# A planned kernel: keeping VectorE and GpSimd apart on their shared port, in the plan and by semaphores

## The chip, the cores and the metric

The kernel runs on one core of one Trainium2 chip. The metric is the device time of one execution in microseconds (us). The profile's span, from first to last instruction, is about 2 us shorter than that time. In the first call, whose chip the record does not name, the runs of one kernel lie within 0.5%. The experiments ran on two chips, called the second and the third below, which were noisier, so small differences are given with 95% intervals. A run more than 1.5% above the fastest of its kernel is called slow.

## The reference, cut to what matters

An attention with a decaying state makes `y`; reshaped to 3072 rows of 384, it is the input of a feed-forward block.

```python
for t in range(S):                                   # B=4, H=8, S=768, D=48
    cur = einsum('bhd,bhe->bhde', u[None] * kt, vt)
    y[:, :, t] = einsum('bhd,bhde->bhe', rt, state + cur)
    state = w[None, :, :, None] * state + einsum('bhd,bhe->bhde', kt, vt)
x = y.transpose(0, 2, 1, 3).reshape(B * S, H * D)    # 3072 x 384
h = x @ w_in                                         # 384 x 2048
r = maximum(h, 0.0); g = r * r
out = g @ w_out                                      # 2048 x 384
```

## The kernel before

The kernel cuts attention into 24 units of 128 steps (6 stretches of the sequence, 4 batches). Per unit, five elementwise products of 128x384 (`kw`, `rw`, `rk`, `rku`, `dv`, and a smaller `smo`) may run on VectorE or on GpSimd. Two units feed one of 12 feed-forward pairs: eight groups of six matmuls for the first product ("first products"), a relu, a square, and then groups of four matmuls of the second ("second products").

The order of instructions on every engine is not written by hand. A planner, which is Python that runs when the kernel is built, gives each operation a start, an engine and a place in that engine's queue, from assumed durations. The chip keeps the order of each queue, but not the planned times: an instruction starts as soon as it is first in its queue and its operands are there.

The port rule of the planner before, the fitted priorities and one product:

```python
s = max(t, free[e])
if e == "V" and o.port and lastP is not None and lastP[1] > s:
    s = lastP[1]
elif e == "P" and lastV is not None and lastV[2] and lastV[1] > s >= lastV[0]:
    s = lastV[1]
late = s + o.swift * cost + (away if i else 0.0)
...
if o.dma is not None:
    ...
    if e == "P":
        lastP = (s, s + 0.3, False)
...
ORDER = {"kvm": 1.49, "m1": -2.25, "m2": 0.04, ...}      # added to every operation's key
EARLY = {"dv": -1.05, "relu": 13.78, "trk": -22.02, ...} # added in the first units alone
AWAY, SWIFT, SWIFT_UNITS = 0.05, 1.0, 10
...
q["rku"] = op(f"rku{n}", both(0.96, 0.48), K + 2, [q["rk"], o_ub], ..., port=True)   # GpSimd 0.96, VectorE 0.48
...
for o in placed:
    ...
    o.emit(o.by)
```

`port=True` marks products with both inputs in SBUF, the memory that the engines share. When VectorE has such a product while GpSimd has one too, one of them takes longer (1.35 instead of 0.55 us in the trace below); that is called a collision, an overlap or a port conflict here. The rule looks at the last operation of the other engine only: once VectorE has been given another operation, an earlier port product is forgotten.

Of the kernel before, what the change touches and what calls it, by code (L numbers as in the profile page):

```python
# [11 lines left out]
ALU = mybir.AluOpType  # L12
# [3 lines left out]
class Op:  # L16


    def __init__(self, name, eng, key, deps, takes, emit, lat, port, dma):
        self.name, self.eng, self.key, self.deps, self.takes = name, eng, key, deps, takes  # L20
        self.emit, self.lat, self.port, self.dma = emit, lat, port, dma
        self.start = self.end = self.by = self.ins = None
        self.gap, self.swift = 0.0, 0.0


class Buf:
# [8 lines left out]
        return max(u.end for u in self.users) + 0.1  # L35


def schedule(ops, depth, limits, free, away, stalls, warm_until=0.0):
    rings = {r: [] for r in depth}
    banks = [None] * 8  # L40
    free = dict(free)
# [6 lines left out]
            succ.setdefault(d, []).append(o)  # L48
    ready = [o for o in ops if need[o] == 0]
    placed = []  # L50
    lastP = lastV = None
    base, queue = {}, []

    def ring_time(o):
# [49 lines left out]
    while ready:  # L104
        best = None
        for o in ready:
            t = base.get(o)
            if t is None:
                t = 0.0
                for d, lat in o.deps:  # L110
                    t = max(t, d.end + (d.lat if lat is None else lat))
                base[o] = t
            if best is not None and t > best[0][0]:
                continue
            r = ring_time(o)
            if r is None:
                continue
            t = max(t, r)
            if best is not None and t > best[0][0]:
                continue  # L120
            chosen = ()
            if any(bf.ring in limits for bf in o.takes):
                got = pick_banks(o, t)
                if got is None:
                    continue
                t, chosen = got
            pick = None
            for i, (e, cost) in enumerate(o.eng.items()):
                s = max(t, free[e])
                if e == "V" and o.port and lastP is not None and lastP[1] > s:  # L130
                    s = lastP[1]
                elif e == "P" and lastV is not None and lastV[2] and lastV[1] > s >= lastV[0]:
                    s = lastV[1]
                late = s + o.swift * cost + (away if i else 0.0)
                if pick is None or late < pick[0]:
                    pick = (late, s, e)
            rank = (pick[1], o.key)
            if best is None or rank < best[0]:
                best = (rank, o, pick[2], chosen)
        if best is None:  # L140
            raise RuntimeError("stuck: " + ", ".join(o.name for o in ready[:20]))
        (s, _), o, e, chosen = best
        cost = o.eng[e]
        o.start, o.by = s, e
        o.gap = s - free[e]
        if o.dma is not None:
            pre, xf, post = o.dma
            x0 = max(s + pre, free["D"])
            x1 = x0 + xf + sum(d for at, d in stalls if x0 <= at < x0 + xf)
            free["D"], o.end = x1, x1 + post  # L150
            free[e] = s + cost
            if e == "S":
                queue.append(x1)
                if len(queue) > 2:
                    free[e] = max(free[e], queue[-3])
            if e == "P":
                lastP = (s, s + 0.3, False)
        else:
            o.end = s + cost
            free[e] = o.end  # L160
            if e == "P":
                lastP = (s, o.end, o.port)
            elif e == "V":
                lastV = (s, o.end, o.port)
        for bf in o.takes:
            if bf.ring not in limits:
                bf.slot = len(rings[bf.ring]) % depth[bf.ring]
                rings[bf.ring].append(bf)
        for bf, i in chosen:
            bf.slot = i  # L170
            banks[i] = bf
        ready.remove(o)
        placed.append(o)
        for n in succ.get(o, ()):
            need[n] -= 1
            if need[n] == 0:
                ready.append(n)
# [6 lines left out]
def kernel(  # L184
# [30 lines left out]
    WARM0 = 5  # L215
    NT = 10
    NDVE = 24
    ORDER = {"kvm": 1.49, "m1": -2.25, "m2": 0.04, "mask": -2.59, "relu": -0.41, "sbo": 5.28, "sma": 3.15, "smo": -0.97, "sq": 1.01, "vb": 4.47, "ym": -0.91, "yt": -4.84}
    EARLY = {"dv": -1.05, "kw": 0.33, "m1": 1.78, "m2": 1.76, "osb": 5.37, "relu": 13.78, "rkT": -3.42, "rku": 0.23, "sma": -6.8, "trk": -22.02, "trr": 5.21, "vb": -6.7, "ym": -10.21, "yt": 2.72}
    AWAY, SWIFT, SWIFT_UNITS = 0.05, 1.0, 10  # L220
    PIECES = (0, 1, 2, 4, 6, 8)
    AHEAD = 4
    BEFORE, BEHIND = 4, 1
# [130 lines left out]

    o_wb = op("wb", {"W": 0.0}, -60, [], lambda e: None, lat=0.75)
    o_row = op("row", {"W": 0.0}, -59, [], lambda e: None, lat=0.0)
    o_ubp = op("ubp", {"T": 1.3}, -58, [o_row], spread_u, takes=[ub_p], lat=0.25)
    o_wcol = op("wcol", {"T": 1.4}, -57, [o_ubp], column_w, takes=[wc_p], lat=0.25)
    o_ln = op("lnw", {"A": 0.5}, -56, [o_wb], lambda e: nc.scalar.activation(lnw, wb, AF.Ln))
    o_wk = op("wk", {"A": 0.5}, -55, [o_ln],  # L360
              lambda e: nc.scalar.activation(wk.rearrange("p h d -> p (h d)"), lnw, AF.Exp, scale=ek))
# [28 lines left out]
    def load(n, nm, gate=None):  # L390
        q = units[n]
        src = {"kt": k, "rt": r, "vt": v}[nm]
        c, b = q["c"], q["b"]

        def f(e):
            q[nm].ins = nc.sync.dma_start(
                out=q["T"](nm), in_=src[b, :, c * C : (c + 1) * C, :].rearrange("h t d -> t h d"))
            if gate is not None:
                tc.add_manual_dep(q[nm].ins.ins, gate.ins.ins.name, LANDED)

        deps = [(gate, 0.05)] if gate is not None else []
        if loads:
            deps.append((loads[-1], -40.0))
        q[nm] = op(f"{nm}{n}", {"S": 0.55}, PACE * (n - AHEAD), deps, f, takes=[q["_" + nm]], lat=0.05, dma=(0.65, 0.95, 1.8))
        loads.append(q[nm])

    o_win, o_wout = [None] * NH, [None] * NH
# [1 line left out]
    def weights(i, which, gate):  # L409
        lo, hi = PIECES[i], PIECES[i + 1]  # L410
        sl = slice(lo * 256, hi * 256) if which == "in" else slice(lo * 2, hi * 2)

        def f(e):
            if which == "in":
                o.ins = nc.gpsimd.dma_start(out=w_in_sb[:, :, sl], in_=w_in_v[:, :, sl])
            else:
                o.ins = nc.gpsimd.dma_start(out=w_out_sb[:, sl, :], in_=w_out_v[:, sl, :])
            if gate is not None:
                tc.add_manual_dep(o.ins.ins, gate.ins.ins.name, LANDED)

        o = op(f"w_{which}{i}", {"P": 0.77}, -5 + 0.1 * i, [(gate, 0.05)] if gate is not None else [(w_ops[-1], -40.0)], f, lat=0.05,
               dma=(1.45, (1.0 if which == "in" else 1.12) * (hi - lo), 1.4))
        for j in range(lo, hi):
            (o_win if which == "in" else o_wout)[j] = o
        return o
# [152 lines left out]
    for j in range(NU // L):  # L578
# [5 lines left out]
        for i, q in enumerate(us):  # L584
            if q["n"] >= NT:
                o_xt.append(op(
                    f"xt{q['n']}", {"S": 1.2}, PACE * q["n"] + 4.4, [q["yb"]],
                    lambda e, XT=XT, i=i, q=q: nc.sync.dma_start_transpose(out=XT()[:, :, i, :], in_=q["T"]("yb")),
                    takes=[xt] if i == 0 else [], uses=[q["_yb"]] + ([xt] if i else []), lat=0.05, dma=(0.9, 0.6, 1.1)))
                continue  # L590
            o_xt.append(op(f"xt{q['n']}", {"A": 0.37, "V": 0.28}, PACE * q["n"] + 4.5, [q["yt"]],
                           copy(lambda XT=XT, i=i: XT()[:, :, i, :], q["ytp"]),
# [6 lines left out]
        for f in range(NH):  # L599
# [22 lines left out]
            def square(e, f=f, gr=gr, G=G):  # L622
                src = make["gr"][gr.slot]
                dst = G()[:, 2 * f : 2 * f + 2].rearrange("p z b t -> p (z b t)")
                if e == "A":
                    nc.scalar.activation(dst, src, AF.Square)  # L626
                else:
                    NOW[e].tensor_tensor(dst, src, src, ALU.mult)  # L628

            o_r = op(f"relu.{j}.{f}", {"V": 0.6, "A": 0.5}, key - 1, [o_m], relu, uses=[gr, h])  # L630
            o_s = op(f"sq.{j}.{f}", {"A": 0.55, "P": 1.02}, key - 1, [o_r], square, uses=[gr, g], port=True)
# [20 lines left out]
    for o in ops:  # L652
        if o.key < PACE * SWIFT_UNITS:
            o.swift = SWIFT

    for o in ops:
        kind, _, num = o.name.partition(".")
        if not num:
            kind, num = o.name.rstrip("0123456789"), o.name[len(o.name.rstrip("0123456789")):]
        elif kind.rstrip("0123456789") == "mask":  # L660
            kind, num = "mask", kind[4:]
        ffn = kind in ("m1", "m2", "relu", "sq")
        first = int((num.partition(".")[0]) or 0) < (3 if ffn else 6)
        o.key += ORDER.get(kind, 0.0) + (EARLY.get(kind, 0.0) if first else 0.0)

    placed = schedule(
        ops, depth, limits,
        free={"T": 4.0, "V": 4.2, "A": 4.4, "P": 2.3, "D": 2.7, "S": 1.2, "W": 3.2},
        stalls=[(18.3 + 12.4 * i, 1.0) for i in range(16)],
        away=AWAY, warm_until=WARM_UNTIL)  # L670
    for o in placed:
        if o.by == "T" and o.gap > 0 and o.start < WARM_UNTIL:
            warm(int(o.gap * WARM_FILL / 0.2133))
        o.emit(o.by)


# [28 lines left out]
```

## Time and profile before

| | before |
|---|---|
| time | 182.15 us median of 3 runs (182.13 to 182.28) |
| span of the profiled run | 181.0 us (its time was 183.06 us) |
| TensorE, VectorE, GpSimd busy | 93%, 78%, 61% |
| first first-product, first second-product | 22.1 us, 38.8 us |
| port products on VectorE | 28, of which 17 pairs overlap a GpSimd product |

The head of the profile page of the kernel before: busy us of each engine, then busy tenths in 40 slices of 4.5 us, and the granted TensorE clock in tenths.

```profile
span 181.0 us, 4349 instructions
...
PE 168.6 (93%) x1646; PEld 122.0 (67%) x1646; DVE 141.6 (78%) x257; ACT 111.4 (62%) x221; POOL 110.6 (61%) x131
...
PE   6995698999999989999999898999999999999992
...
PEclk9999879999999999999999999999999999999999
```

After about 40 us TensorE is practically always busy. The idle time is in the ramp, slices 4 and 5 (about 14 to 23 us), where the granted clock falls a little later. The Trainium skill, "TensorE: Matmul & The Clock Gate", section "What's actually happening", says that a hardware activity monitor sets the clock by how busy TensorE has been. This trace agrees: the stretches view gives a granted clock of 0.66 for 20 to 25 us, at the end of the idle slices and just after, and 1.00 for the next 5 us.

The timeline of VectorE (DVE) and GpSimd (POOL) in the ramp of the kernel before: start us, duration us, engine, line, operation, result and inputs.

```profile
11.71 0.69 DVE L332 TENSOR_TENSOR krp<-rt,wr 128x384 bf16<-128x384 f32 x1
12.32 1.35 DVE L332 TENSOR_TENSOR rku<-rk,ub 128x384 f32<-128x384 f32 x1
...
17.70 0.97 DVE L332 TENSOR_TENSOR krp<-rt,wr 128x384 bf16<-128x384 f32 x1
...
19.83 1.06 DVE L332 TENSOR_TENSOR rku<-rk,ub 128x384 f32<-128x384 f32 x1
20.82 0.55 DVE L332 TENSOR_TENSOR krp<-kt,wk 128x384 bf16<-128x384 f32 x1
```

```profile
11.94 1.32 POOL L332 TENSOR_TENSOR rk<-rt,kt 128x384 f32<-128x384 f32 x1
...
17.24 1.01 POOL L332 TENSOR_TENSOR rk<-rt,kt 128x384 f32<-128x384 f32 x1
18.20 1.32 POOL L332 TENSOR_TENSOR krp<-rt,wr 128x384 bf16<-128x384 f32 x1
```

The product at 20.82 has no GpSimd neighbour and takes 0.55 us. The `rku` at 12.32 lies beside the GpSimd product of 11.94 to 13.26 and takes 1.35 us, ending 0.41 us after it; the GpSimd product, which itself began beside the `krp` of 11.71, takes 1.32 instead of 1.00 us. Over the run the 28 port products of VectorE take 5.0 us more than at 0.55 us each (0.35 for the small one), and GpSimd's 2.5 us more than undisturbed.

The last piece to know is the stretch of the chain of waits around 100 us, where TensorE is held by transposes made by DMA. Columns: start, us, what.

```profile
98.90 4.00 DMA rkT<-krp
102.95 0.40 PE bank L531 x8
103.35 0.43 PE bank L635 x2
...
104.14 5.11 DMA rkT<-krp
109.30 0.40 PE bank L531 x8
```

### The profile page before, as it was taken

The numbers are of one execution on the slowest core, as the hardware profiler recorded it, in microseconds if no ns is written. First come the engines' busy times: TensorE is split into PE (matmuls) and PEld (weight loads), VectorE is DVE, ScalarE is ACT, GpSimd is POOL, SyncE is SP. The second block draws the span as 40 slices with busy tenths as digits, with TensorE's granted clock in tenths as the row PEclk, the third lists the DMA queues.
The fourth block names the chain that finished last, engine by engine and source line by source line (L and its number), as shares of the span: only waits on it lengthen the run. The fifth ranks groups of instructions, "written<-read, shape, count | busy, mean of one in ns | idle before, by whom it ended". The sixth has DMA issues, their size and how long they took to land.

```text
span 181.0 us, 4349 instructions
## 1 busy us (share of the span) xinstructions
PE 168.6 (93%) x1646; PEld 122.0 (67%) x1646; DVE 141.6 (78%) x257; ACT 111.4 (62%) x221; POOL 110.6 (61%) x131
## 2 busy tenths in 40 slices
PE   6995698999999989999999898999999999999992
PEld 2653476876776667777787576687677776877760
DVE  6899977998799988868588586797898686765640
ACT  2545369992494968986666465667476465453641
POOL 2199519801089999999999798899897000010200
PEclk9999879999999999999999999999999999999999
DMA  4999999997799799999694988898994320120202
GB/s 96 208 196 150 180 170 182 159 181 143 153 230 218 169 197 220 203 202 207 131 202 120 217 172 215 164 215 188 204 167 119 94 83 22 24 88 22 87 4 87
DMA packets 103254, 27.55 MB, mean 152 GB/s; under 512 B 96065, under 2 KB 103234, under 8 KB 103234
## 3 DMA queue, kind: packets, MB, share of 16 engines
q1 hardware_dynamic: 99088, 24.13, 62.4%
q0 software_dynamic: 4128, 3.15, 12.1%
q8 instruction: 13, 0.21, 0.5%
q14 instruction: 7, 0.06, 0.1%
q10 hardware_dynamic: 18, 0.00, 0.0%
HBM read 20.65 MB, written 4.72 MB: 140 GB/s over the span
## 4 chain that ended last, share of the span: by engine, by line
PE 50%; POOL 22%; DVE 10%; issue 7%; DMA 5%; ACT 3%; POOLq 0%; DVEq 0%
PE bank L635 22%; PE bank L606 19%; POOL krp L332 8%; DMA rkT<-krp 5%; POOL rku L332 5%; POOL rk L332 4%; POOL dv L332 2%; POOL sm L332 2%; PE bank L531 2%; DVE AT L539 2%; PE bank L325 2%; DVE krp L332 1%; PE bank L476 1%; PE bank L555 1%; PE bank L550 1%
## 5 line engine op out<-in xcount | busy, mean ns | idle before, releaser
L635 PE MATMUL bank<-w_out_sb,g 128*128 128x384 bf16 x384 | 77.9, 326 | 0.0
L606 PE MATMUL bank<-xt,w_in_sb 128*128 128x256 bf16 x576 | 77.1, 276 | 0.3 <-ACT xt L337 0.3
L626 ACT ACTIVATE g<-gr 128x512 bf16<-128x512 f32 x92 | 57.0, 630 | 25.0 <-DVE gr L618 23.9
L606 PEld LDWEIGHTS <-w_in_sb 128*128 128x128 bf16 x576 | 55.3, 99 | 12.9 <-issue 0.6
L618 DVE TENSOR_SCALAR gr<-bank 128x512 f32<-128x512 f32 x68 | 46.5, 689 | 20.7 <-PE bank L606 18.5
L635 PEld LDWEIGHTS <-g 128*128 128x128 bf16 x384 | 34.5, 98 | 15.6
L539 DVE TENSOR_TENSOR AT<-bank,smask 128x512 bf16<-128x512 f32 x48 | 30.8, 683 | 3.1 <-PE bank L531 2.8
L332 POOL TENSOR_TENSOR dv<-vb,du 128x384 f32<-128x384 bf16 x20 | 16.6, 832 | 19.5 <-DVE du L461 19.4
L332 POOL TENSOR_TENSOR krp<-kt,wk 128x384 bf16<-128x384 f32 x19 | 19.8, 1040 | 9.7 <-DMA kt<-in_k_dram 6.3
L332 POOL TENSOR_TENSOR rk<-rt,kt 128x384 f32<-128x384 f32 x22 | 23.0, 1047 | 0.1
L620 ACT ACTIVATE gr<-bank 128x512 f32<-128x512 f32 x28 | 16.2, 596 | 9.9 <-PE bank L606 9.0
L628 POOL TENSOR_TENSOR g<-gr 128x512 bf16<-128x512 f32 x4 | 4.2, 1039 | 29.4 <-DVE gr L618 29.4
L337 ACT COPY osb<-bank 128x384 f32<-128x384 f32 x21 | 9.4, 479 | 14.4 <-PE bank L635 14.4
L563 DVE TENSOR_TENSOR yb<-bank,dv 128x384 bf16<-128x384 f32 x24 | 13.3, 553 | 5.5 <-PE bank L555 4.4
L332 POOL TENSOR_TENSOR rku<-rk,ub 128x384 f32<-128x384 f32 x17 | 17.3, 1023 | 0.2
L523 ACT CAST sb_all<-sm 64x192 bf16<-64x192 f32 x40 | 13.9, 346 | 4.9 <-DVE sm L520 1.8
L332 POOL TENSOR_TENSOR krp<-rt,wr 128x384 bf16<-128x384 f32 x16 | 16.7, 1046 | 0.0
L337 ACT CAST vb<-vt 128x384 bf16<-128x384 f32 x24 | 12.1, 505 | 3.0 <-DMA vt<-in_v_dram 1.7
L461 DVE TENSOR_REDUCE du<-rku 128x8 f32<-128x384 f32 x24 | 13.0, 543 | 0.2
L555 PE MATMUL bank<-vb,AT 128*128 128x48 bf16 x192 | 11.3, 184 | 1.5 <-DVE AT L539 1.3
L555 PEld LDWEIGHTS <-AT 128*128 128x128 bf16 x192 | 9.8, 97 | 3.4 <-issue 1.3
L531 PE MATMUL bank<-rkT 48*128 48x128 bf16 x192 | 9.9, 222 | 2.3 <-DMA rkT<-krp 1.8
(55 smaller groups left out, 146.2 us busy)
## 6 DMA issues: line engine op xcount, KB each, us to landing
kt<-in_k_dram SPq DMA_DIRECT2D x24, 192.0 KB, 3.5
rt<-in_r_dram SPq DMA_DIRECT2D x24, 192.0 KB, 3.7
vt<-in_v_dram SPq DMA_DIRECT2D x24, 192.0 KB, 3.9
out_dram<-osb SPq DMA_DIRECT2D x24, 192.0 KB, 2.5
w_in_sb<-in_moe_w_in_dram POOLq DMA_DIRECT2D x3, 384.0 KB, 8.4
w_out_sb<-in_moe_w_out_dram POOLq DMA_DIRECT2D x3, 384.0 KB, 9.6
w_in_sb<-in_moe_w_in_dram POOLq DMA_DIRECT2D x2, 192.0 KB, 4.5
w_out_sb<-in_moe_w_out_dram POOLq DMA_DIRECT2D x2, 192.0 KB, 4.6
```

The source lines that it names most:

```text
L332: return lambda e: NOW[e].tensor_tensor(dst(), a(), b_(), f)
L337: nc.scalar.copy(dst(), src())
L523: halves(lambda e, rows, i, sb=sb, sm=sm: nc.scalar.copy(SM(sb)[rows, :, i, :], SM(sm)[rows])),
L531: nc.tensor.matmul(out=psv(at[i], NP, C)[:, p, :], lhsT=T("rkT")[rows, 1, p, :], rhs=T("rkT")[rows, 0, p, :], start=True, stop=True,)
L539: lambda e, T=T, i=i, x=x: nc.vector.tensor_tensor(T("AT")[:, i], psv(x, NP, C), smask[:, None, :].to_broadcast([128, NP, C]), ALU.mult),
L555: nc.tensor.matmul(out=t[:, p, i, :], lhsT=T("AT")[:, i, p, :], rhs=T("vb")[:, 2 * p + i, :], start=st is None, stop=True, skip_group_chec ...
L563: lambda e, T=T, y_p=y_p: nc.vector.tensor_tensor(T("yb"), psv(y_p, HD), T("dv").rearrange("t h d -> t (h d)"), ALU.add),
L606: nc.tensor.matmul(out=psv(h, 2, L * C)[:, z], lhsT=w_in_sb[:, kk, (2 * f + z) * 128 : (2 * f + z + 1) * 128], rhs=XT()[:, kk].rearrange(" ...
L618: nc.vector.tensor_scalar(dst, src, 0.0, None, ALU.max)
L620: nc.scalar.activation(dst, src, AF.Relu)
L626: nc.scalar.activation(dst, src, AF.Square)
L635: nc.tensor.matmul(out=psv(o_p, dm), lhsT=G()[:, 2 * f + z, i, :], rhs=w_out_sb[:, 2 * f + z, :], start=(f == 0 and z == 0), stop=(f == NH ...
```

## The change

The intent: the planner should never place a port product of VectorE and a GpSimd instruction at the same time, and where the plan puts a GpSimd instruction after such a product, a semaphore should hold GpSimd to it. With this went three other edits: the fitted priorities are dropped, the preference for the engine that finishes sooner ends at unit 6 instead of 10, and some planned durations are set anew. The core of the diff, with cuts marked:

```diff
-    lastP = lastV = None
+    heldP, heldV, portV = [], [], None
...
-                if e == "V" and o.port and lastP is not None and lastP[1] > s:
-                    s = lastP[1]
-                elif e == "P" and lastV is not None and lastV[2] and lastV[1] > s >= lastV[0]:
-                    s = lastV[1]
+                if e == "V" and o.port:
+                    for a, b in heldP[-6:]:
+                        if s < b and s + cost > a:
+                            s = b
+                elif e == "P":
+                    for a, b in heldV[-6:]:
+                        if s < b and s + cost > a:
+                            s = b + 0.1
...
+        if e == "P" and portV is not None:
+            o.after, portV = portV, None
...
-                lastP = (s, s + 0.3, False)          # a DMA issued from GpSimd
+                heldP.append((s, free[e]))
...
+            if e == "T" and s < cold and cost < 1.0:  # TensorE before 10 us
+                cost = max(cost * 1.7, cost + 0.2)
...
-    ORDER = {...}
-    EARLY = {...}
-    AWAY, SWIFT, SWIFT_UNITS = 0.05, 1.0, 10
+    SLACK_FROM, HOLD, STORE_WAIT, Y_WAIT, RK_WAIT = 5.0, 0.0, 0.0, 0.0, 0.0
+    AWAY, SWIFT, SWIFT_UNITS = 0.05, 1.0, 6
...
-    o_ubp = op("ubp", {"T": 1.3}, ...      o_wcol = op("wcol", {"T": 1.4}, ...
+    o_ubp = op("ubp", {"T": 1.5}, ...      o_wcol = op("wcol", {"T": 1.65}, ...
-    loads dma=(0.65, 0.95, 1.8)   y transposes dma=(0.9, 0.6, 1.1)   stalls from 18.3
+    loads dma=(0.65, 0.92, 1.8)   y transposes dma=(0.9, 0.5, 1.1)   stalls from 20.0
...
-        o.emit(o.by)
+        o.made = o.emit(o.by)
+        if o.after is not None:
+            tc.add_manual_dep(o.made.ins, o.after.made.ins.name, LANDED)
```

(The four lines on durations are drawn together from several places.) `HOLD` and the three waits are new knobs for late transfers; all are zero here.

More of the change, by code (lines that the diff above doesn't have):

```diff
@@ L22, in __init__ @@
         self.start = self.end = self.by = self.ins = None
-        self.gap, self.swift = 0.0, 0.0
+        self.after = None
+        self.gap, self.swift, self.wait, self.hold = 0.0, 0.0, 0.0, 0.0
 class Buf:
@@ L35, in free_at, with schedule @@
         return max(u.end for u in self.users) + 0.1
-def schedule(ops, depth, limits, free, away, stalls, warm_until=0.0):
+def schedule(ops, depth, limits, free, away, stalls, warm_until=0.0, cold=0.0):
     rings = {r: [] for r in depth}
@@ L110, in schedule @@
                 for d, lat in o.deps:
-                    t = max(t, d.end + (d.lat if lat is None else lat))
+                    t = max(t, d.end + (d.lat + d.hold + o.wait if lat is None else lat))
                 base[o] = t
@@ L161, in schedule @@
             if e == "P":
-                lastP = (s, o.end, o.port)
-            elif e == "V":
-                lastV = (s, o.end, o.port)
+                heldP.append((s, o.end))
+            elif e == "V" and o.port:
+                heldV.append((s, o.end))
+                portV = o
         for bf in o.takes:
@@ L217 @@
     NDVE = 24
-    ORDER = {"kvm": 1.49, "m1": -2.25, "m2": 0.04, "mask": -2.59, "relu": -0.41, "sbo": 5.28, "sma": 3.15, "smo": -0.97, "sq": 1.01, "vb": 4.47, "ym": -0.91, "yt": -4.84}
-    EARLY = {"dv": -1.05, "kw": 0.33, "m1": 1.78, "m2": 1.76, "osb": 5.37, "relu": 13.78, "rkT": -3.42, "rku": 0.23, "sma": -6.8, "trk": -22.02, "trr": 5.21, "vb": -6.7, "ym": -10.21, "yt": 2.72}
-    AWAY, SWIFT, SWIFT_UNITS = 0.05, 1.0, 10
+    SLACK_FROM, HOLD, STORE_WAIT, Y_WAIT, RK_WAIT = 5.0, 0.0, 0.0, 0.0, 0.0
+    AWAY, SWIFT, SWIFT_UNITS = 0.05, 1.0, 6
     PIECES = (0, 1, 2, 4, 6, 8)
@@ L356 @@
     o_row = op("row", {"W": 0.0}, -59, [], lambda e: None, lat=0.0)
-    o_ubp = op("ubp", {"T": 1.3}, -58, [o_row], spread_u, takes=[ub_p], lat=0.25)
-    o_wcol = op("wcol", {"T": 1.4}, -57, [o_ubp], column_w, takes=[wc_p], lat=0.25)
+    o_ubp = op("ubp", {"T": 1.5}, -58, [o_row], spread_u, takes=[ub_p], lat=0.25)
+    o_wcol = op("wcol", {"T": 1.65}, -57, [o_ubp], column_w, takes=[wc_p], lat=0.25)
     o_ln = op("lnw", {"A": 0.5}, -56, [o_wb], lambda e: nc.scalar.activation(lnw, wb, AF.Ln))
@@ L403, in load @@
             deps.append((loads[-1], -40.0))
-        q[nm] = op(f"{nm}{n}", {"S": 0.55}, PACE * (n - AHEAD), deps, f, takes=[q["_" + nm]], lat=0.05, dma=(0.65, 0.95, 1.8))
+        q[nm] = op(f"{nm}{n}", {"S": 0.55}, PACE * (n - AHEAD), deps, f, takes=[q["_" + nm]], lat=0.05, dma=(0.65, 0.92, 1.8))
         loads.append(q[nm])
@@ L419, in f @@
                 tc.add_manual_dep(o.ins.ins, gate.ins.ins.name, LANDED)
+            return o.ins
         o = op(f"w_{which}{i}", {"P": 0.77}, -5 + 0.1 * i, [(gate, 0.05)] if gate is not None else [(w_ops[-1], -40.0)], f, lat=0.05,
@@ L588 @@
                     lambda e, XT=XT, i=i, q=q: nc.sync.dma_start_transpose(out=XT()[:, :, i, :], in_=q["T"]("yb")),
-                    takes=[xt] if i == 0 else [], uses=[q["_yb"]] + ([xt] if i else []), lat=0.05, dma=(0.9, 0.6, 1.1)))
+                    takes=[xt] if i == 0 else [], uses=[q["_yb"]] + ([xt] if i else []), lat=0.05, dma=(0.9, 0.5, 1.1)))
                 continue
@@ L627, in square @@
                 else:
-                    NOW[e].tensor_tensor(dst, src, src, ALU.mult)
+                    return NOW[e].tensor_tensor(dst, src, src, ALU.mult)
             o_r = op(f"relu.{j}.{f}", {"V": 0.6, "A": 0.5}, key - 1, [o_m], relu, uses=[gr, h])
@@ L654 @@
             o.swift = SWIFT
-    for o in ops:
-        kind, _, num = o.name.partition(".")
-        if not num:
-            kind, num = o.name.rstrip("0123456789"), o.name[len(o.name.rstrip("0123456789")):]
-        elif kind.rstrip("0123456789") == "mask":
-            kind, num = "mask", kind[4:]
-        ffn = kind in ("m1", "m2", "relu", "sq")
-        first = int((num.partition(".")[0]) or 0) < (3 if ffn else 6)
-        o.key += ORDER.get(kind, 0.0) + (EARLY.get(kind, 0.0) if first else 0.0)
+        if o.dma is not None and o.key > PACE * SLACK_FROM:
+            o.hold = HOLD
+            if o.name.startswith("st"):
+                o.wait = STORE_WAIT
+            elif o.name.startswith("xt"):
+                o.wait = Y_WAIT
+            elif o.name.startswith("rkT"):
+                o.wait = RK_WAIT
     placed = schedule(
@@ L668 @@
         free={"T": 4.0, "V": 4.2, "A": 4.4, "P": 2.3, "D": 2.7, "S": 1.2, "W": 3.2},
-        stalls=[(18.3 + 12.4 * i, 1.0) for i in range(16)],
-        away=AWAY, warm_until=WARM_UNTIL)
+        stalls=[(20.0 + 12.4 * i, 1.0) for i in range(16)],
+        away=AWAY, warm_until=WARM_UNTIL, cold=10.0)
     for o in placed:
```

## The prediction

> **What bounds the kernel now.** The stretches view shows TensorE busy 60.0 of 60 us in 40–60, 80–100 and 120–140 together, and about 58 of 60 in 60–80, 100–120 and 140–160 (19.4, 18.2, 20.0). So the steady part is TensorE's. At the rate of the timeline (0.65 us per first product of six matmuls, 0.33 us per two of the second), 96 and 192 of these plus about 27 us for attention are some 152 us of work. So 29 us of the 181 us span are not work. Some 19 lie before 38 us (16 of 96 first products started by then), about 2.5 us near 99–110 us, where the chain of waits shows TensorE behind two key transposes by DMA that took 4.0 and 5.1 us, and 4 us at the end.
>
> The ramp is VectorE's: busy 9.78 of 10 us in 10–20 us, with most of the chain on it.
>
> **What the change does.**
> 1. Port conflicts. By form, VectorE's SBUF–SBUF products have means of 0.65 (krp), 0.86 (rku) and 0.91 us (dv); undisturbed ones in the timeline take 0.55. Excess: 13×0.10 + 7×0.31 + 4×0.35 ≈ 5 us in the whole run. About 2.5 us of it lies between 11 and 21 us (rku 1.35, dv 1.18, krp 0.97, rku 1.06), beside GpSimd products of 1.32 instead of 0.96–1.00. The Trainium skill, "SBUF — State Buffer", section "Who interferes with whom", says that a VectorE instruction with two SBUF inputs contends with a GpSimd instruction reading SBUF; this trace agrees (1.35 against 0.55). Planned apart, part of the 2.5 us is filled with other work. Worth 1–1.5 us of the ramp.
> 2. The semaphores. Perhaps 20–30 GpSimd instructions get one. GpSimd idles 4.7 and 6.4 us in the ramp, so there they cost little. From 57 to 140 us it is nearly full, but few VectorE products stand there. Hardly on the path.
> 3. GpSimd's weight-DMA issues, 4 us in a row at 13.2 and at 29.3, now bar VectorE's products in the plan for their whole length rather than 0.3 us each. In the trace krp at 31.16 took 0.55 during such an issue, so part of this caution is unneeded: up to 1 us lost.
> 4. The fitted priorities are dropped. With plain keys feed-forward work comes earlier among units 3–5, which feeds TensorE but delays attention: between −1 and +2 us.
> 5. The preference for the faster finisher ends at unit 6 rather than 10: VectorE (17.95 of 20 in 40–60) loses some 10 products, GpSimd (10.3 of 20) gains them and saturates earlier. TensorE is full there; no gain.
> 6. DMA times in the plan barely change: the 2.5 us at 99–110 may move rather than vanish.
>
> **Prediction.** 180.5 us, 1% faster: −1.5 (ports) −0.5 (order, clock) +0.5 (caution). Range 176.8 to 184.8. Chances: faster by over 2% 0.25, within 2% 0.62, slower 0.13.
>
> **What would show it.** Step 1: rku, krp and dv on VectorE at 0.55 mean, GpSimd products at 0.96–1.00, and the first second-layer matmul before its present 38.8 us. Step 2: GpSimd waits for VectorE's krp/rku/rk in the list of waits, below 2 us in total. Step 5: fewer VectorE products (28 now), GpSimd busy above 110.6 us. Step 6: waits of TensorE on the transposed keys still 1–3 us.
>
> **What would make it wrong.** Plain priorities starving TensorE in the ramp or in mid-run (slower by 3–6 us); GpSimd's added work making attention arrive late; or a truer plan removing TensorE's idle time throughout the ramp (faster by 4 us).

## The result, and the profile after

| | before | after |
|---|---|---|
| time, median | 182.22 us (4 runs) | 180.26 us (4 runs, 180.10 to 180.91) |
| ratio, first call | | 0.9897 (0.987 to 0.9924) |
| ratio, second chip (run again as control) | | 0.9956 (0.9903 to 1.0008) |
| span of the profiled run | 181.0 us | 178.3 us |
| first first-product, first second-product | 22.1, 38.8 us | 20.1, 33.9 us |
| overlapping pairs | 17 | 0 |

The profiled run of the kernel before was 0.8 us slower than its median, so the spans differ by more (2.7 us) than the medians (2.0 us). A ratio is the mean time of one kernel's fast runs over the mean of the other's of the same rounds, so it is not quite the ratio of the medians.

The page of the kernel after, the same lines:

```profile
span 178.3 us, 4338 instructions
...
PE 167.8 (94%) x1644; PEld 121.0 (68%) x1646; DVE 134.0 (75%) x249; ACT 114.8 (64%) x221; POOL 115.4 (65%) x139
...
PE   6998796999999999999999999699999999999991
...
PEclk9999999999999999999999999999999999999998
```

The same engines in the ramp of the kernel after, VectorE first:

```profile
12.01 0.55 DVE L341 TENSOR_TENSOR rku<-rk,ub 128x384 f32<-128x384 f32 x1
...
17.30 0.55 DVE L341 TENSOR_TENSOR krp<-rt,wr 128x384 bf16<-128x384 f32 x1
...
19.56 0.55 DVE L341 TENSOR_TENSOR rku<-rk,ub 128x384 f32<-128x384 f32 x1
20.02 0.55 DVE L341 TENSOR_TENSOR krp<-rt,wr 128x384 bf16<-128x384 f32 x1
```

```profile
11.03 1.00 POOL L341 TENSOR_TENSOR krp<-kt,wk 128x384 bf16<-128x384 f32 x1 [1.26 <-DMA kt<-in_k_dram]
...
20.67 0.99 POOL L341 TENSOR_TENSOR rk<-rt,kt 128x384 f32<-128x384 f32 x1 [3.61 <-DVE krp L341]
```

Every port product of VectorE now takes 0.55 us (22 of them, excess 0.05 us in total), and GpSimd's 128x384 products with f32 inputs take 1.00 to 1.01. The GpSimd product at 20.67 shows the semaphore at work: GpSimd stood idle for 3.61 us until VectorE's `krp` (20.02 to 20.57) was over. The Trainium skill, "SBUF — State Buffer", section "Who interferes with whom", says that a VectorE instruction with two SBUF inputs contends with a GpSimd instruction that reads SBUF. The two traces agree: 0.55 us apart, up to 1.35 us together.

The list of waits of the kernel after, GpSimd's waits for port products of VectorE: us in total, times, longest.

```profile
POOL krp L341 <- DVE krp L341: 6.8, 1, 6.8
...
POOL rk L341 <- DVE krp L341: 3.6, 1, 3.6
POOL rku L341 <- DVE rk L341: 2.5, 1, 2.5
...
POOL w_in_sb L424 <- DVE rku L341: 1.0, 1, 1.0
```

These sum to 13.9 us of idle GpSimd, all before 38 us, and GpSimd has 1% of the chain of waits. In the kernel before no such wait is listed, and GpSimd has 22%. But a wait in this list is not yet a cost of the semaphore. The list of the same kernel without the semaphores (first experiment) has nearly the same idle time at three of the four places, where GpSimd waits for a load or for its own input instead:

```profile
POOL krp L341 <- DMA rt<-in_r_dram: 7.0, 1, 7.0
...
POOL rku L341 <- DVE rk L341: 2.9, 1, 2.9
...
POOL w_in_sb L424 <- DMA vt<-in_v_dram: 1.1, 1, 1.1
```

Only the wait of 3.6 us at 20.67 is gone there, so that one alone is time in which a semaphore held GpSimd; without it GpSimd idles 3.3 us longer before its next `dv` (6.4 instead of 3.1 us).

The chain of waits of the kernel after where TensorE is still held in mid-run:

```profile
112.28 0.57 DVE AT L549
112.84 2.92 DMA xt<-yb
...
115.90 2.78 PE bank L616 x24
```

It is another transpose by DMA, of y instead of the keys, and TensorE is idle 1.42 us for it; in the kernel before it was idle 2.33 us after 60 us (0.52, 0.76 and 1.06).

How far the work has come by 60 us is read from the stretches view of the two product lines: us, then busy us and count of matmuls and of weight loads, the clock, the DMA share and GB/s. Kernel before, first products and then second products:

```profile
0.00:60.00 60.00, 18.65 (x135) 13.34 (x136) 0.97 0.96 174
...
0.00:60.00 60.00, 14.83 (x76) 6.61 (x76) 0.97 0.96 174
```

Kernel after:

```profile
0.00:60.00 60.00, 17.57 (x138) 12.71 (x138) 1.00 1.00 185
...
0.00:60.00 60.00, 16.43 (x84) 7.52 (x84) 1.00 1.00 185
```

At six and four matmuls a group this is 41.5 groups before and 44.0 after. A group of either kind takes 0.65 us in the chain, so the kernel after is 1.6 us ahead. Together with 0.9 us less idle time later this makes 2.5 us of the 2.7 us between the spans.

### The profile page after: what moved, and what is told of

It is laid out like the page before. It is cut to its first block, busy times and chain, and to the rows that moved or that the text cites. A ratio compares the mean times of both kernels' runs of the same rounds, so it can differ in the third digit from the quotient of the medians.

```text
span 178.3 us, 4338 instructions
## 1 busy us (share of the span) xinstructions
PE 167.8 (94%) x1644; PEld 121.0 (68%) x1646; DVE 134.0 (75%) x249; ACT 114.8 (64%) x221; POOL 115.4 (65%) x139
## 4 chain that ended last, share of the span: by engine, by line
PE 78%; DVE 8%; DMA 8%; issue 2%; ACT 1%; POOL 1%; DVEq 0%
PE bank L645 34%; PE bank L616 33%; DMA w_in_sb<-in_moe_w_in_dram 4%; PE bank L541 4%; PE bank L565 2%; DMA wb<-in_w_dram 2%; PE bank L560 2%; DVE AT L549 2%; DMA xt<-yb 2%; PE bank L486 1%; PE bank L506 1%; DVE gr L628 1%; POOL w_in_sb L424 1%; DVE krp L341 1%; DVE du L471 1%
## 5 line engine op out<-in xcount | busy, mean ns | idle before, releaser
L636 ACT ACTIVATE g<-gr 128x512 bf16<-128x512 f32 x90 | 56.6, 630 | 33.9 <-DVE gr L628 32.6
L616 PE MATMUL bank<-xt,w_in_sb 128*128 128x256 bf16 x576 | 76.0, 273 | 2.0 <-DMA xt<-yb 1.4
L616 PEld LDWEIGHTS <-w_in_sb 128*128 128x128 bf16 x576 | 54.4, 98 | 14.3 <-issue 1.5
L341 POOL TENSOR_TENSOR krp<-rt,wr 128x384 bf16<-128x384 f32 x19 | 19.2, 1008 | 6.8 <-DVE krp L341 6.8
L341 POOL TENSOR_TENSOR krp<-kt,wk 128x384 bf16<-128x384 f32 x20 | 20.1, 1006 | 5.1 <-PE bank L565 3.8
L341 POOL TENSOR_TENSOR rku<-rk,ub 128x384 f32<-128x384 f32 x21 | 21.1, 1006 | 2.7 <-DVE rk L341 2.5
L630 ACT ACTIVATE gr<-bank 128x512 f32<-128x512 f32 x29 | 17.2, 593 | 8.0 <-PE bank L616 7.5
L341 POOL TENSOR_TENSOR rk<-rt,kt 128x384 f32<-128x384 f32 x19 | 19.1, 1005 | 3.7 <-DVE krp L341 3.6
L638 POOL TENSOR_TENSOR g<-gr 128x512 bf16<-128x512 f32 x6 | 6.3, 1042 | 23.4 <-DVE gr L628 23.4
L341 POOL TENSOR_TENSOR dv<-vb,du 128x384 f32<-128x384 bf16 x19 | 15.8, 834 | 5.4 <-DVE du L471 4.9
L524 DVE TENSOR_TENSOR sm<-bank,sm 64x192 f32<-64x192 f32 x32 | 11.3, 353 | 1.6 <-PE bank L506 1.2
L346 ACT COPY osb<-bank 128x384 f32<-128x384 f32 x18 | 7.9, 481 | 4.7 <-PE bank L645 4.1
```

Source lines behind the costliest of these rows:

```text
L341: return lambda e: NOW[e].tensor_tensor(dst(), a(), b_(), f)
L346: nc.scalar.copy(dst(), src())
L616: nc.tensor.matmul(out=psv(h, 2, L * C)[:, z], lhsT=w_in_sb[:, kk, (2 * f + z) * 128 : (2 * f + z + 1) * 128], rhs=XT()[:, kk].rearrange(" ...
L630: nc.scalar.activation(dst, src, AF.Relu)
L636: nc.scalar.activation(dst, src, AF.Square)
```

## The experiments

The first theory: the collisions cost the ramp its time, and the planner's rule takes them away. Rivals: the semaphores do it; the dropped priorities do it; the new durations do it; or the plan after is one lucky draw. All twelve runs, the control among them, gave correct results. The planner was also asked for its own numbers, which needs no chip:

```
                              planned end   planned overlaps   port products on VectorE   semaphores
before                        169.4 us      18                 28                         0
before + new rule             173.0 us       0                 29                         0
after                         170.7 us       0                 22                         8
after + fitted priorities     171.6 us       0                 23                         9
after + old durations         171.6 us       0                 19                         6
```

(The planned end is that of the last engine's work. Of the 18 planned overlaps, 13 are with a GpSimd product and 5 with an issue of a weight DMA; measured overlaps below count products only.) The old plan counted these as free, so its 169.4 us could not be kept: by 20 us VectorE's products ran 3.5 us behind it (`dv2` was planned at 20.5 and started at 24.0). In the kernel after they ran 0.2 us behind.

### Semaphores taken out of the kernel after

```diff
-        o.made = o.emit(o.by)
-        if o.after is not None:
-            tc.add_manual_dep(o.made.ins, o.after.made.ins.name, LANDED)
+        o.emit(o.by)
```

> The kernel after, every instruction in the same order, without its 8 added semaphores. Theory (the plan alone keeps the two engines apart; the semaphores only guard against drift): 180.0 to 180.8 us, at most 2 overlaps of a VectorE product with a GpSimd one, VectorE products still 0.55 us. Rival (the semaphores are what keeps them apart): 5 or more overlaps, products of 0.65 us and longer in the first 40 us, 181 us or more.

Measured: ratio 0.9978 (0.9925 to 1.0031), median 182.04 us, from 180.19 to 185.46; six overlaps. The timeline of GpSimd, then of VectorE, of this run:

```profile
16.77 1.28 POOL L341 TENSOR_TENSOR rk<-rt,kt 128x384 f32<-128x384 f32 x1
18.14 1.19 POOL L341 TENSOR_TENSOR rku<-rk,ub 128x384 f32<-128x384 f32 x1
```

```profile
17.71 0.77 DVE L341 TENSOR_TENSOR rk<-rt,kt 128x384 f32<-128x384 f32 x1
18.40 1.34 DVE L341 TENSOR_TENSOR krp<-kt,wk 128x384 bf16<-128x384 f32 x1
```

With the semaphore this GpSimd `rk` had started at 20.67. Without it, it starts 3.9 us sooner, since its operands are there and its queue is free, and it meets VectorE's products. So the rival is right as to what keeps the engines apart: the plan alone doesn't. What that is worth in time is not resolved: the interval overlaps that of the control on the same chip. The profiled run was a slow one; the collisions are taken from it, its length is not. Its ramp speaks against a gain from the semaphores: with six collisions it has started as much by 60 us as the kernel after (first products, then second):

```profile
0.00:60.00 60.00, 17.57 (x138) 12.70 (x138) 1.00 1.01 185
...
0.00:60.00 60.00, 16.25 (x84) 7.44 (x84) 1.00 1.01 185
```

That is 44.0 groups in both.

### Semaphores alone, on the plan before

The kernel before with nothing else added:

```diff
+        if e == "P" and portV is not None:
+            o.after, portV = portV, None
...
                 lastV = (s, o.end, o.port)
+                if o.port:
+                    portV = o
...
-        o.emit(o.by)
+        o.made = o.emit(o.by)
+        if o.after is not None:
+            tc.add_manual_dep(o.made.ins, o.after.made.ins.name, LANDED)
```

> The kernel before, same order and plan, with semaphores that make each first GpSimd instruction after a VectorE port product wait for it. Theory (removing collisions by waiting gives no time back, the plan must place the work elsewhere): 182 to 183.5 us, since VectorE products behind a GpSimd product in flight are still blocked (excess of VectorE's port products 2 to 4 us instead of 5.0). Rival (the lock itself is the loss, the semaphore alone removes it): 180.0 to 181.0 us with an excess below 1 us.

Measured: ratio 1.0008 (0.9951 to 1.0065); overlaps 8 instead of 17, excess of VectorE's products 2.3 instead of 5.0 us; first first-product at 20.0 us, but the first second-product only at 37.6 us; clock 1.00 throughout. This is what the theory expected. Collisions can be turned into waits without a gain. It also shows that a full clock alone doesn't bring the gain: the dip of the kernel before is gone here and the time is the same. That the dip has no part in the gain is not shown (see the account below).

### The rule alone, on the kernel before

```diff
-                if e == "V" and o.port and lastP is not None and lastP[1] > s: ...
-                elif e == "P" and lastV is not None and lastV[2] and ...
+                if e == "V" and o.port:
+                    for a, b in heldP[-6:]: ...
+                elif e == "P":
+                    for a, b in heldV[-6:]: ...
```

> The kernel before with the planner's new exclusion rule alone (fitted priorities, old times, preference to unit 10 all kept; no semaphores). Theory (the gain is the port rule's): 179.8 to 181.2 us, overlaps down from 17 to 0 to 3. Rival (the gain comes from the plain priorities and the re-timed plan; the fitted priorities belong to the old plan and are wrong under the new rule): 182 to 185 us in spite of no overlaps.

Measured: ratio 1.0101 (1.0051 to 1.015), slower, and 17 overlaps as before. My theory failed here. The plan had none; the chip had as many as ever. GpSimd and VectorE in the ramp of this run:

```profile
11.85 1.32 POOL L336 TENSOR_TENSOR rk<-rt,kt 128x384 f32<-128x384 f32 x1
...
17.15 1.01 POOL L336 TENSOR_TENSOR rk<-rt,kt 128x384 f32<-128x384 f32 x1
```

```profile
12.24 1.35 DVE L336 TENSOR_TENSOR rku<-rk,ub 128x384 f32<-128x384 f32 x1
...
17.37 1.22 DVE L336 TENSOR_TENSOR dv<-vb,du 128x384 f32<-128x384 bf16 x1
```

The GpSimd product that started at 17.15 was planned for 20.4. A gap in a plan is nothing that a queue knows of. The rule makes the plan longer (173.0 us) to keep gaps, and without semaphores the chip closes the gaps and collides all the same.

### The fitted priorities alone taken out of the kernel before

```diff
-    ORDER = {...}
-    EARLY = {...}
-        o.key += ORDER.get(kind, 0.0) + (EARLY.get(kind, 0.0) if first else 0.0)
```

> The kernel before with the fitted priorities taken out, nothing else. Theory (priorities are worth little by themselves; collisions stay): 181.5 to 184 us, 12 to 20 overlaps. Rival (dropping the fitted priorities is the gain): 180.0 to 181.0 us with the overlaps still there.

Measured: ratio 1.0045 (1.0003 to 1.0087), 20 overlaps. Dropping them is no gain by itself; on the old plan it is a small loss.

### The kernel after, once more

No edit: a control on the second chip.

> The kernel after once more, as the control for this chip and this call: 179.8 to 181.5 us, ratio to the kernel before 0.985 to 0.995, no overlaps, spread of its runs below 1.5 us. If the spread is as wide as it was without the semaphores (180.2 to 185.5), that spread was not theirs.

Measured: ratio 0.9956 (0.9903 to 1.0008), 179.90 to 183.82 us, no overlaps, span 179.4 us. The ratio is a little above what was expected and the spread is wider, so the wide spread without semaphores wasn't theirs alone.

### Rule and semaphores together on the kernel before

```diff
+                    for a, b in heldP[-6:]: ...            # the rule, as above
+                    for a, b in heldV[-6:]: ...
+            tc.add_manual_dep(o.made.ins, o.after.made.ins.name, LANDED)
```

> The kernel before with the new rule and the semaphores, fitted priorities, preference to unit 10 and old times kept. The rule alone left 17 overlaps, because GpSimd ran up to 3.2 us ahead of its plan into VectorE's products. Theory A (rule and semaphore work only together, and the fitted priorities still cost): 0 to 4 overlaps, VectorE's excess below 1 us, 181.3 to 183.3 us. Theory B (rule plus semaphore is the whole gain): 179.8 to 181.0 us. Theory C (priorities are the whole): 183 us or more, as with the rule alone (183.9).

Measured: ratio 1.0128 (1.0084 to 1.0172), 184.11 us, 4 overlaps, excess 1.7 us. Theories A and B both miss; C had the time but not the reason. Four collisions instead of 17, and slower than ever: the ramp of this longer plan is worse (37.2 groups by 60 us, with a granted clock of 0.83 from 20 to 40 us). So taking the collisions away isn't enough; the plan that does so must also be good.

### Fitted priorities put back into the kernel after

```diff
+    ORDER = {...}                                          # as in the kernel before
+    EARLY = {...}
+        o.key += ORDER.get(kind, 0.0) + (EARLY.get(kind, 0.0) if first else 0.0)
```

> The kernel after with the fitted priorities put back, all else of the change kept. Theory A (they were fitted to the old plan and do not suit this one): 181.0 to 183.0 us, overlaps still at most 2. Theory B (priorities do not matter): within 0.5 us of the control.

Measured: ratio 1.0049 (0.9998 to 1.0101), against 0.9956 for the control; no overlaps; 40.5 groups by 60 us instead of 44.0. This speaks for theory A, that they don't suit the new plan, but the intervals of the two kernels overlap a little. Where the groups are lost can be read: both kernels have 8.0 at 30 us, and by 35 us this one has 11.0 and the kernel after 14.2. In these 5 us its granted clock is 0.66, after TensorE had been busy for 3.23 of 5 us from 25 us on (3.60 in the kernel after). The kernel after, then this run (busy us and instructions of TensorE, its weight loads, VectorE, ScalarE and GpSimd; then the clock):

```profile
30.00:35.00 5.00, 5.00 (x63) 4.11 (x61) 4.50 (x10) 4.36 (x8) 4.95 (x7) 1.00 0.91 130
```

```profile
30.00:35.00 5.00, 4.11 (x25) 2.92 (x25) 2.93 (x7) 2.68 (x5) 4.07 (x6) 0.66 0.99 130
```

A clock of 0.66 for 5 us is worth 1.7 us at full clock, by my estimate some 2.6 of the 3.2 groups lost there at 0.65 us each.

### Old durations put back into the kernel after

```diff
-"ubp" 1.5, "wcol" 1.65, loads 0.92, y transposes 0.5, stalls from 20.0, cold=10.0
+"ubp" 1.3, "wcol" 1.4,  loads 0.95, y transposes 0.6, stalls from 18.3, cold=0.0
```

> The kernel after with the planner's old durations (loads, transposes, first matmuls, no slower TensorE before 10 us, old phase of the transfer stalls). Theory (the new durations mend little, the semaphores absorb the drift): 180.3 to 181.8 us, overlaps at most 3. Rival (the gain is that of truer durations): 182 us or more.

Measured: ratio 1.0115 (1.0062 to 1.0167), median 183.50 us, one overlap, 40.3 groups by 60 us. The rival is right in that the durations matter, and this is the largest loss that undoing any single part made (1.6% against the control, and the intervals are apart). Here the clock in the ramp is full. Which of the six numbers does it was not tried, and that it is their truth, rather than just another plan, is not shown: two plans of one planned end differ by 1.4% below.

### Preference for the faster finisher kept to unit 10

```diff
-    AWAY, SWIFT, SWIFT_UNITS = 0.05, 1.0, 6
+    AWAY, SWIFT, SWIFT_UNITS = 0.05, 1.0, 10
```

> The kernel after with the preference for the faster finisher kept to unit 10 instead of 6: 37 port products on VectorE instead of 22, 13 semaphores instead of 8, the planner's own end 170.5 instead of 170.7. Theory (TensorE is full from 40 us, so this part of the change gains nothing): within 0.7 us of the kernel after, that is a ratio of 0.988 to 1.000 to the kernel before. Rival (sparing VectorE after unit 6 was part of the gain): 1.003 or more. In both no overlaps.

Measured: ratio 0.9943 (0.9891 to 0.9994), 37 port products on VectorE, 2 short overlaps (0.4 us together). This edit of the change is worth nothing that shows in time. Its profile has 41.8 groups by 60 us, but that is not typical: the profiled run alone had a dip of the clock at 30 to 35 us (mean clock 0.991; the four other fast runs 1.000, with spans of 178.9 to 179.9 us against its 180.1).

### One microsecond of slack for transfers

```diff
-    SLACK_FROM, HOLD, ... = 5.0, 0.0, ...
+    SLACK_FROM, HOLD, ... = 5.0, 1.0, ...
```

> The kernel after with the planner told that every transfer after unit 5 lands 1.0 us later; the planned end is the same, 170.7. In the kernel after the first products run 2.1 us behind plan at number 48 and 4 us at number 64, about when TensorE waits 1.4 us for a transposed y. Theory (late transfers in a fixed order cost the rest): that jump is below 1 us, spread of the runs below 2 us, ratio 0.980 to 0.990. Rival (the lag comes from elsewhere): no change, 0.990 to 1.000, TensorE still waiting over 1 us for a transfer.

Measured: ratio 0.984 (0.9791 to 0.9889), median 179.64 us, from 178.90 to 180.59, no slow run; span 177.6 us. TensorE's waits for transfers in this run, from the list of waits:

```profile
PE bank L616 <- DMA w_in_sb<-in_moe_w_in_dram: 1.2, 1, 1.2
...
PE bank L645 <- DMA w_out_sb<-in_moe_w_out_dram: 0.5, 1, 0.5
```

Only the two waits for weights before 40 us are left; none is for a transposed tensor, and TensorE has no idle gap over 0.15 us between 60 and 170 us. The lag behind the plan grows by 0.4 us from first product 48 to 64, where it grew by 1.9 us in the kernel after. It is the fastest kernel and beats both medians of the kernel after, but the two were timed in different calls, and the intervals of 0.984 and 0.9897 overlap: how much the slack gives over the kernel after is not shown. Nor is it shown that slack is what removes the waits: the kernel after with fitted priorities has none without slack, and the next run has 2.63 us of them with it.

### Priorities fitted anew, with the slack

Four searches of about 4,000 sets each were made on the planner alone, for the shortest planned end with `HOLD` at 1.0; the outcome of one was run.

```diff
+    ORDER = {'m1': 0.55, 'm2': 2.21, 'sma': -0.98, 'vb': 1.5, 'yt': -2.57, 'yb': -4.46}
+    EARLY = {'m2': -0.52, 'rkT': 2.23, 'sma': -4.08, 'trk': -10.52, 'ym': -19.28, 'sq': -11.97, ...}
-    SLACK_FROM, HOLD, ... = 5.0, 0.0, ...
+    SLACK_FROM, HOLD, ... = 5.0, 1.0, ...
-    AWAY, SWIFT, SWIFT_UNITS = 0.05, 1.0, 6
+    AWAY, SWIFT, SWIFT_UNITS = 0.079, 1.0, 9
```

> Priorities fitted anew to the new planner with the 1.0 us of transfer slack: planned end 169.1 instead of 170.7, 33 port products on VectorE. Theory (once collisions are held off, the chip follows the plan, so that a plan 1.6 us shorter is about 1.6 us faster): ratio 0.972 to 0.986, no overlaps. Rival (below 2 us the plan's length says nothing of the chip's): 0.988 to 1.005.

Measured: ratio 0.9966 (0.9902 to 1.0029), span 181.2 us; five overlaps, and TensorE idle 2.63 us after 60 us for transposes. The theory failed: a plan 1.6 us shorter was 1.3% slower than the plain plan with slack (0.9966 against 0.984 in the same call).

### A change of plan without a reason

```diff
-    AWAY, SWIFT, SWIFT_UNITS = 0.05, 1.0, 6
+    AWAY, SWIFT, SWIFT_UNITS = 0.1, 1.0, 6
```

> A change of plan without a reason: the penalty for an operation's second choice of engine is 0.10 instead of 0.05 us; planned end 170.7 as before, 20 port products on VectorE, another order on every engine. It measures how far plans of equal length lie apart. If the change was a gain of method: ratio 0.985 to 1.000. If the kernel after was one lucky draw among equals: 1.003 or more.

Measured: ratio 0.998 (0.9934 to 1.0025), 43.5 groups by 60 us, TensorE idle 2.53 us after 60 us, all but a little for transposed y. The ramp is as good as that of the kernel after; the mid-run is worse. The ratio lies in the range of a gain of method, but its interval holds 1.000, so the rival of a lucky draw is not excluded. Against the kernel after (0.9956 and 0.9897 on other chips) the difference of 0.2 to 0.8% is not resolved, since the kernel after differs from itself by 0.6%. In one call, two plans with a planned end of 170.7 us, this one and the one with slack, lie 1.4% apart (0.998 and 0.984, intervals apart); by the account below it is which transposes come late.

### What the runs have in common

Two numbers of each profile nearly give its span: the groups of matmuls started by 60 us (the ramp), and TensorE's idle gaps over 0.15 us between 60 and 170 us (late transfers). The last column is 177.6 us, the span of the kernel with slack, plus 0.65 us for each group short of its 43.5, plus the idle time.

```
                              groups by 60 us   idle 60-170 us   span    sum of the account
before                        41.5              2.33             181.0   181.2
before + semaphores           41.8              1.47             180.0   180.2
before + rule                 42.0              1.50             180.5   180.1
before, plain priorities      41.0              0.96             180.4   180.2
before + rule + semaphores    37.2              0.92             183.2   182.7
after                         44.0              1.42             178.3   178.7
after, control                43.8              1.64             179.4   179.1
after + fitted priorities     40.5              0.00             179.3   179.6
after + old durations         40.3              0.24             180.3   179.9
after, preference to 10       41.8              1.25             180.1   180.0
after + transfer slack        43.5              0.00             177.6   177.6
after + new priorities, slack 43.3              2.63             181.2   180.3
after, null shift             43.5              2.53             180.0   180.1
```

The account holds within 0.9 us, and within some 0.5 us but for one. It is an account of single profiled runs, not a proof. The run without semaphores is left out, because its profile is a slow run; with 44.0 groups and 3.96 us idle it would come to 181.2 us against 183.2. In both misses the granted clock from 100 to 140 us is 0.96, which the account doesn't count.

Two things follow that the first theory did not expect. The ramp doesn't go by the collisions: 17 of them go with 41.5 and 42.0 groups, six with 44.0 (in the slow run), none with 40.5 and 44.0. And the clock is a rival that no run isolates. In the call of the control, the fast runs of the kernel before had a mean clock of 0.986 and a mean span of 179.9 us, those of the kernel after 0.997 and 179.2 us. Within the kernel before, the six runs with a clock of 0.981 or less had a mean span of 180.2 us, the six others 179.6 us. So, as an estimate, about 0.6 of the 0.7 us between the kernels there goes with the clock. The clock in turn goes with the ramp: from 10 to 20 us TensorE is busy for 8.73 of 10 us in the kernel after and 6.71 in the kernel before. It is not enough by itself, as the runs with old durations and with semaphores alone show, which have a full clock in the ramp and no gain.

## Why the prediction was right or wrong

The time was right: 180.5 us was forecast and 180.26 us measured, within 2% as thought most likely. In the control it was 181.58 us, with a ratio whose interval reaches 1.0008, so how large the gain is stays open. The steps fared as follows.

1. **Port conflicts.** The sizes of the collision were right: VectorE's products fell to 0.55 us, GpSimd's to 1.00 us, the first second-product came at 33.9 instead of 38.8 us, and the ramp's lead of 1.6 us is near the net 1.5 us of the sum. What failed is "Planned apart, part of the 2.5 us is filled with other work. Worth 1–1.5 us of the ramp", taken as a gain of the rule: the rule alone left 17 overlaps and cost 1%, and rule with semaphores on the old settings cost 1.3%. The ramp's lead was seen where the rule went with plain priorities and new durations; putting back either lost about 3.5 groups, in the first case mostly within a dip of the clock. Without the semaphores the lead was there in full with six collisions (44.0 groups), so the end of the collisions is not what made it. How much the rule alone gives within the kernel after was not tried by taking it out there, and stays open.
2. **Semaphores.** Forecast: 20 to 30, with waits below 2 us. Measured: 8, with 13.9 us of waits for VectorE's port products in the list, of which 3.6 us are the semaphores' doing. Both sizes were wrong; that it costs nothing was right (GpSimd has 1% of the chain). They are what makes the chip keep the plan's gaps, as the two runs of rules without semaphores show; that this is worth time is not shown.
3. **Caution around weight-DMA issues.** Not isolated. Between 12.5 and 16.8 us VectorE had no port product, but was filled with other work apart from 0.6 us of waiting, so no loss is seen; whether there is one stays open. That the caution is unneeded was nearly right: in the traces of all kernels here, 31 port products of VectorE ran beside such an issue and no GpSimd product, and 28 of them took no longer than undisturbed.
4. **Fitted priorities.** "Between −1 and +2 us": taking them out of the old kernel gave +0.45%, putting them into the new one about +0.9%. The range held, though the second interval overlaps the control's; that the sign depends on the plan they were fitted to was not seen.
5. **Preference to unit 6.** "No gain" was right as far as the intervals tell (0.9943 with it undone, 0.9956 and 0.9897 for the kernel after). The loss of "some 10 products" was 6 for the whole change; by this edit alone it was 15 (37 to 22). GpSimd's busy time rose to 115.4 us as said.
6. **Transfers and durations.** "DMA times in the plan barely change" passed over the planner's other new durations, and was the largest error: with the old durations back the ratio went from 0.9956 to 1.0115. "May move rather than vanish" was right: the wait moved from two key transposes at 102 and 108 us (1.8 us) to one transpose of y at 114.5 us (1.42 us). In the sum it stood as zero; the account gives −0.9 us, and the null shift shows that this term can as well be +0.2 us.

So the total came out right with one term of the right size, the ramp, from a different mixture of causes than written, and with one term, the mid-run, that was set to zero and came to −0.9 us. That the sum fits is partly luck. What made the ramp's lead stays open between the priorities, the durations and the clock that goes with them.

## What to carry to other kernels

A static plan becomes an order of queues, and its gaps are lost unless a semaphore carries them: check on the trace whether the engine that should wait does wait, and don't expect the plan's exclusion to be kept by itself. Count collisions and time apart: here a kernel with six of them had the same ramp as one with none, and a wait in a list is a cost only if it is gone when its cause is taken out. Before comparing, look at the granted clock of each run; here it went with most of the difference in one call. A plan that is 1 us shorter says little when two plans of equal length differ by 1.4% on the chip, and fitting priorities to the new plan brought no gain. Slack for transfers in the plan (here 1 us, with no loss in planned length) is worth trying where an engine is full and runs a fixed order: that kernel was the fastest here (ratio 0.984), though its gain over the kernel after is not resolved.

## What the Trainium skill lacked or had wrong

- "SBUF — State Buffer" has the rule for two SBUF inputs but no durations for a pair of elementwise products: a 128x384 product on VectorE went from 0.55 to 1.35 us, and the GpSimd product beside it, which had begun beside an earlier product of VectorE, from 1.00 to 1.32 us, so either side can lose.
- The same page has a VectorE instruction with two SBUF inputs contend only with a GpSimd instruction that reads SBUF. Of the 31 port products in all traces that ran, for 0.1 us or more, beside nothing on GpSimd but an issue of a weight DMA, 28 agree. Three do not: in the kernel before, the `dv` product at 15.28 us took 1.18 us (issues from 13.21 to 17.22 us) and the `krp` product at 32.23 us 0.76 us, and with the priorities taken out the `dv` product at 15.28 us took 1.09 us. No run isolates the cause.
- None of the pages that I used gives the delay when GpSimd is ordered after VectorE by a semaphore: GpSimd started 0.10 us after the product of VectorE that it waited for (20.57 to 20.67 us).
